# Two-layer decode attention on one core: PE's loop from step 1, the order of layouts and wo matmuls in step 31, and the type of the last transpose

## The chip, the core and the metric

The kernel runs on one core of a Trainium2 chip. The core has a matrix engine (TensorE, PE in the profile; its weight loads are the rows PEld), a vector engine (VectorE, DVE), a scalar engine (ScalarE, ACT), GpSimd (POOL) and a synchronisation engine (SyncE, SP) that here issues nearly all transfers. 16 DMA engines move data between memory (HBM) and the on-chip SBUF; each transfer is spread over all of them. PE writes its results to PSUM, from where DVE and ACT read them. The metric is device time of one execution in microseconds (us), given as a median of several runs; less is better.

## The reference

Two independent attention layers, A and B, each decode one token (one query row) against a cache of 8192 keys and values in 32 heads of 128. Their results are put side by side.

```python
D, H, Sk, Dh = 512, 32, 8192, 128          # for A and for B alike
q = (x @ wq).reshape(1, 1, H, Dh)           # x: 1 x 512, wq: 512 x 4096
scores = einsum("bhqd,bhkd->bhqk", q, k_cache) * Dh ** -0.5
p = softmax(scores, axis=-1)
o = einsum("bhqk,bhkd->bhqd", p, v_cache)
y = o.reshape(1, 1, H * Dh) @ wo            # wo: 4096 x 512
out = concatenate([y_A, y_B], axis=-1)      # 1 x 1024
```

All inputs and the output are bf16. The caches of both layers together are 268 MB, and the profile counts 285.21 MB read from HBM.

## The kernel before

A step `n` handles two heads of one layer: steps 0 to 15 are A's 32 heads, steps 16 to 31 are B's. The 128 partitions hold the two heads, 64 partitions each; a partition holds 128 keys of 128 elements. K and V of a step are one transfer of 4 MB each (`load_k`, `load_v`, issued on SP; V of step 31 in two halves), into two K buffers and two V buffers. K of step n+2 waits until PE has read K of step n (`red_done`), V of step n+2 until PE has used V of step n (`pv_done`).

One step goes through these operations, with the lines at which the profile shows them:

- `plan_mul` (L292, DVE): four multiplications of K, in place, by the query.
- `plan_red` (L301, PE): two groups of 16 matmuls with the identity, 512 columns each, which add up the products of a key into PSUM (`rps`); `plan_sr` (L310, DVE) finishes the sum to one score per key.
- `plan_max`, `plan_gmax` (L316, L322, L325): the maximum per head; `plan_exp` (L335 on PE, L339 and L346 on ACT) spreads it over the partitions and takes the exponentials.
- in the following step: `plan_sum` (L351, PE; L354, DVE) adds up the exponentials of the step before and takes the reciprocal; `plan_pv` (L367, PE) multiplies them with V in 128 matmuls of two columns; `plan_o` (L377, DVE) scales the result into `oD`.

So PE's order in step n is: sum of step n-1, reduction of step n, first half of the product with V of step n-1, maximum of step n, second half of that product, spread of step n. A last pass, step 32, has only the sum and the product of step 31.

The projection with wq (`plan_q`, L274 on PE, L282 on ACT) stands at the beginning for A and at the beginning of step 1 for B.

The projection with wo needs the result in another arrangement. `plan_relayout(a, g)` makes it for a group of heads: DVE writes a masked copy `zb` (L402), one PE matmul with a selection matrix turns it into `misc` (L406), DVE copies that to `o2` (L408). `plan_wo(a, g)` (L419, PE) then multiplies with the group's part of wo, four matmuls of one column per head, all 32 heads adding into `qyp`. A's 32 heads are one group; B's are groups of 16, 8, 4, 2 and 2 heads. A's layout and wo matmuls and the first three layouts of B stand at the head of step 31; B's last two layouts follow `plan_o` of steps 30 and 31, B's wo matmuls come at the very end. A's wo lies in the buffer `wbuf` from step 12 on. B's wo is loaded into the same buffer in five transfers (`load_wo`), which SP issues once A's wo matmuls are done (`wo_done[0]`). `plan_y` (L426, DVE) copies a layer's result to `yT`, for A behind the second multiplication of step 31. `plan_out` turns both with one PE matmul against the identity (L430), DVE copies the result (L433) and SP stores it.

The order on each engine is the order in which the plan's functions are called. `_Plan.op` appends an instruction to an engine's list, `_Plan.wait` a wait for a semaphore's count, left out when the engine has already waited for that count or a higher one. Four engines get their lists written out. PE's list is cut at `marks`: steps below `L0` are written out, steps `L0` to `L1 - 1` become a loop with two steps per round (`_emit_loop`), and the rest is written out again. In the loop a wait whose count grows from round to round is made against a register that is raised each round. With `L0 = 3` and `L1 = 31` these are 14 rounds, and every round must have the same instructions and waits.

Of the kernel before, what the change touches and what calls it, by code (L numbers as in the profile page):

```python
# [8 lines left out]
BF16 = mybir.dt.bfloat16  # L9
F32 = mybir.dt.float32  # L10

P = 128
# [11 lines left out]
class _Plan:  # L24
# [6 lines left out]
    def wait(self, eng, mark):  # L31
        if mark is None:
            return
        ctr, val = mark
        if val <= 0 or self.waited.get((eng, ctr.name), 0) >= val:
            return
        self.waited[(eng, ctr.name)] = val
        self.prog[eng].append((None, ctr, val))

    def op(self, eng, fn, ctr=None, needs=(), inc=1):  # L40

        for m in needs:
            self.wait(eng, m)
        self.prog[eng].append((fn, ctr, inc))
        if ctr is None:
            return None
        ctr.n += inc
        return ctr, ctr.n


def _emit(e, items):
    for fn, ctr, k in items:
        if fn is None:
            e.wait_ge(ctr.sem, k)
        elif ctr is None:
            fn(e)
        else:
            fn(e).then_inc(ctr.sem, k)


def _emit_loop(e, rounds):


    body = rounds[0]
    for r in rounds[1:]:
        assert len(r) == len(body)
        for (f0, c0, k0), (f1, c1, k1) in zip(body, r):
            assert (f0 is None) == (f1 is None) and c0 is c1
            assert f0 is None or k0 == k1
    grow = [rounds[1][i][2] - it[2] if it[0] is None else 0 for i, it in enumerate(body)]  # L70
    for n, r in enumerate(rounds):
        for it, d, base in zip(r, grow, body):
            assert it[0] is not None or it[2] == base[2] + n * d
    regs = {}
    for i, d in enumerate(grow):
        if d:
            regs[i] = e.alloc_register("w%d" % i)
            e.reg_mov(regs[i], body[i][2])
    with e.Fori(0, len(rounds)):
        due = []  # L80
        for i, it in enumerate(body):
            if i in regs:
                e.wait_ge(it[1].sem, regs[i])
                due.append(i)
                continue
            _emit(e, [it])
            if it[0] is not None:
                for j in due:
                    e.reg_add(regs[j], regs[j], grow[j])
                due = []  # L90
        for j in due:
            e.reg_add(regs[j], regs[j], grow[j])


def bass_concat_heads__mha_block_cached__gqa_block_cached__decode_kernel(
# [18 lines left out]
    NA = 2  # L114
# [22 lines left out]
    with ExitStack() as st:  # L137
# [3 lines left out]
        def sb(name, shape, dt):  # L141
            return ec(nc.sbuf_tensor(name, shape, dt))
# [14 lines left out]
        ident = sb("ident", [P, P], BF16)  # L157
        ident_f = sb("ident_f", [P, P], F32)
# [9 lines left out]
        mask = {g: sb("mask%d" % g, [P, P // g], BF16) for g in RG}  # L168
        jsel = {g: sb("jsel%d" % g, [P, g], BF16) for g in RG}
        NQ = NOUT // P  # L170
        yT = sb("yT", [P, NA, NQ], F32)
        out_q = sb("out_q", [NA * NQ, P], BF16)

        def ps(name, shape):
# [9 lines left out]
        pl = _Plan()  # L184
# [15 lines left out]
        def dma(eng, dst, src, c, needs=()):  # L200
            return op(eng, lambda e: e.dma_start(dst, src), c, needs, inc=16)  # L201


        def const(fn, needs=()):
# [5 lines left out]
            out=ident[:], in_=ones_bf[:], pattern=[[1, P]], compare_op=ALU.is_equal,  # L210
            fill=0.0, base=0, channel_multiplier=-1), [i_onesb])
        i_identf = const(lambda e: e.affine_select(
            out=ident_f[:], in_=ones_f[:], pattern=[[1, P]], compare_op=ALU.is_equal,
# [52 lines left out]
        def plan_q(a, j):  # L266

            def mm(e):
                r = None
                for hh in range(2):  # L270
                    for c in range(C):
                        w = wq_sb[a][:, c, 8 * j * Dh:8 * (j + 1) * Dh].rearrange(
                            "p (i h d) -> p i h d", h=2, d=Dh)[:, :, hh, :]
                        r = e.matmul(  # L274
                            qyp[hh * HP:(hh + 1) * HP, :].rearrange("p (i d) -> p i d", d=Dh),
                            xb[:, a, c, hh * HP:(hh + 1) * HP], w,
                            start=(c == 0), stop=(c == C - 1))
                return r
            m = op("PE", mm, c_pe, [x_ready, wq_in[a], qy_free[0]])
            q_done[a] = m  # L280
            n0 = a * PA + 4 * j
            qy_free[0] = op("ACT", lambda e: e.copy(  # L282
                qbc[:, n0:n0 + 4, :].rearrange("p i d -> p (i d)"), qyp[:]), c_act, [m])
            for n in range(n0, n0 + 4):
                qbc_ready[n] = qy_free[0]
# [110 lines left out]
        def plan_relayout(a, g):  # L396
            h0, n = WOG[a][g]
            z = z_n[0] % 2
            z_n[0] += 1
            s = P // n  # L400
            zv = zb[:, z, :].rearrange("p (h s) -> p h s", s=s)
            m = op("DVE", lambda e: e.tensor_tensor(  # L402
                zv, oD[:, a, h0:h0 + n].unsqueeze(2).broadcast_to([P, n, s]),
                mask[n][:, None, :].broadcast_to([P, n, s]), ALU.mult),
                c_dve, [sel_ready[n], o_done[a * PA + (h0 + n) // 2 - 1], z_free.get(z)])
            z_free[z] = op("PE", lambda e: e.matmul(misc[:, 0:n], zb[:, z, :], jsel[n][:],  # L406
                                                    start=True, stop=True), c_pe, [m, misc_free[0]])
            o2_ready[a, g] = misc_free[0] = op("DVE", lambda e: e.tensor_copy(  # L408
                o2[:, a, h0:h0 + n], misc[:, 0:n]), c_dve, [z_free[z]])

        def plan_wo(a, g):

            h0, n = WOG[a][g]

            def mm(e):
                r = None
                for j in range(h0, h0 + n):
                    for i in range(NQ):
                        r = e.matmul(qyp[:, i:i + 1], wo_sb[:, j, i * P:(i + 1) * P],  # L419
                                     o2[:, a, j:j + 1], start=(j == 0 and i == 0),  # L420
                                     stop=(j == H - 1 and i == NQ - 1), skip_group_check=True)
                return r
            wo_done[a] = op("PE", mm, c_pe, [o2_ready[a, g], wo_in[a, g], qy_free[0]])

        def plan_y(a):
            qy_free[0] = op("DVE", lambda e: e.tensor_copy(yT[:, a, :], qyp[:, 0:NQ]), c_dve,  # L426
                            [wo_done[a]])

        def plan_out():
            m = op("PE", lambda e: e.matmul(bmp[0:NA * NQ, 0:P], yT[:].rearrange("p a q -> p (a q)"),  # L430
                                            ident_f[:], start=True, stop=True),
                   c_pe, [qy_free[0], nb_done[NP - 1]])
            m = op("DVE", lambda e: e.tensor_copy(out_q[:], bmp[0:NA * NQ, 0:P]), c_dve, [m])  # L433
            done = dma("SP", out[0].rearrange("o (q n) -> (o q) n", q=NA * NQ), out_q[:], s_out, [m])
            wait("SP", done)


        L0, L1 = 3, 31
        marks = {}

        load_wq(0)
# [5 lines left out]
        for n in range(NP + 1):  # L447
            marks[n] = len(pl.prog["PE"])
            last = n == NP
            if n == L1:  # L450
                plan_relayout(0, 0)
                plan_wo(0, 0)
                for g in range(3):
                    plan_relayout(1, g)
            if n + 1 < NP:
                load_k(n + 1)
            if n == 1:
                for j in range(4):
                    plan_q(1, j)
            if not last:  # L460
                load_v(n, 2 if n == NP - 1 else 1)
            if n == 12:
                load_wo(0, 0)
            if n == NP - 1:
                for g in range(len(WOG[1])):
                    load_wo(1, g)
            if not last:
                plan_mul(n, 0)
                plan_mul(n, 1)
            if n == L1:  # L470
                plan_y(0)
            if n > 0:
                plan_sum(n - 1)
            if not last:
                plan_red(n, 0)
                plan_mul(n, 2)
                plan_mul(n, 3)
                plan_sr(n, 0)
                plan_red(n, 1)
            if n > 0:  # L480
                plan_pv(n - 1, 0, HT)
            if not last:
                plan_sr(n, 1)
                plan_max(n)
                plan_gmax(n)
            if n > 0:
                plan_pv(n - 1, HT, T)
            if not last:
                plan_exp(n)
            if n > 0:  # L490
                plan_o(n - 1)
            if n >= L1:
                plan_relayout(1, n - L1 + 3)
# [44 lines left out]
```

## Time and profile before

| | |
|---|---|
| median of three runs | 675.33 us (673.68, 675.33, 675.58) |
| the profiled execution's own time | 675.39 us |
| its span, first to last instruction | 673.7 us |
| HBM read | 285.21 MB, 423 GB/s over the span |
| busy: PE matmuls, PE weight loads | 469.2 us (70%), 275.7 us (41%) |
| busy: DVE, ACT, POOL | 359.5 us (53%), 43.9 us (7%), 2.1 us |
| mean granted clock of PE | 0.744 of full speed |
| chain that ended last | DMA 61%, PE 26%, DVE 8%, issue 4% |

How to read it: the span is what the profiler saw between the first and the last instruction; the time adds 1.7 us around it. A share of busy time is a mean over the whole span. The chain that ended last is followed back from the last instruction, at each step to what released it; its shares say where the time of that one chain lay. "issue" in it is time in which an engine waited for nothing that the profile shows. In timeline rows the brackets tell how long an engine had been idle before an instruction, and whose end released it. A transfer's time to landing counts from its issue on SP, so it includes the time behind other transfers.

### The profile page before, as it was taken

The numbers are of one execution on the slowest core, as the hardware profiler recorded it, in microseconds if no ns is written. First come the engines' busy times: TensorE is split into PE (matmuls) and PEld (weight loads), VectorE is DVE, ScalarE is ACT, GpSimd is POOL, SyncE is SP. The second block draws the span as 40 slices with busy tenths as digits, with TensorE's granted clock in tenths as the row PEclk, the third lists the DMA queues.
The fourth block names the chain that finished last, engine by engine and source line by source line (L and its number), as shares of the span: only waits on it lengthen the run. The fifth ranks groups of instructions, "written<-read, shape, count | busy, mean of one in ns | idle before, by whom it ended". The sixth has DMA issues, their size and how long they took to land.

```text
span 673.7 us, 12421 instructions
## 1 busy us (share of the span) xinstructions
PE 469.2 (70%) x5712; PEld 275.7 (41%) x5712; DVE 359.5 (53%) x345; ACT 43.9 (7%) x171; POOL 2.1 (0%) x13
## 2 busy tenths in 40 slices
PE   2665887667678766665677787766768875666977
PEld 1223444344444433442344444434444442344637
DVE  1553556566555665615655555656555565655361
ACT  1120000000000000000000000000000000000000
POOL 1000000000000000000000000000000000000000
PEclk9997877666787766776667887766788776678765
DMA  9999999999999999999999999999999999999994
GB/s 374 436 435 431 435 427 426 427 432 436 432 432 434 428 434 426 434 434 434 430 430 432 430 430 434 434 434 432 426 436 428 432 434 432 430 434 427 432 423 182
DMA packets 10547, 285.43 MB, mean 424 GB/s; under 512 B 1186, under 2 KB 1188, under 8 KB 1572
## 3 DMA queue, kind: packets, MB, share of 16 engines
q1 hardware_dynamic: 10528, 285.22, 98.6%
q8 instruction: 10, 0.16, 0.1%
q14 instruction: 5, 0.04, 0.0%
q10 hardware_dynamic: 4, 0.00, 0.0%
HBM read 285.21 MB, written 0.00 MB: 423 GB/s over the span
## 4 chain that ended last, share of the span: by engine, by line
DMA 61%; PE 26%; DVE 8%; issue 4%; ACT 0%; SPq 0%; ACTq 0%
DMA kn<-in_A_k_cache_dram 31%; DMA kn<-in_B_k_cache_dram 30%; PE rps L301 23%; DVE kn L292 7%; PE acc L367 1%; PE qyp L419 1%; PE bmp L335 0%; ACT pt L346 0%; PE misc L406 0%; DVE zb L402 0%; DVE o L408 0%; PE mtp L322 0%; PE bmp L430 0%; PE misc L351 0%; SPq L201 0%
## 5 line engine op out<-in xcount | busy, mean ns | idle before, releaser
L301 PE MATMUL rps<-kn,ident 128*128 128x512 bf16 x1024 | 292.3, 456 | 143.3 <-DVE kn L292 143.3
L292 DVE TENSOR_TENSOR kn<-kn,qbc 128x4096 bf16<-128x4096 bf16 x128 | 286.8, 2284 | 92.1 <-DMA kn<-in_A_k_cache_dram 62.1
L301 PEld LDWEIGHTS rps<-kn,ident 128*128 128x128 bf16 x1024 | 113.6, 114 | 309.7 <-DVE kn L292 141.9
L367 PEld LDWEIGHTS acc<-pt,vn 128*128 128x128 bf16 x4096 | 110.6, 97 | 14.3 <-issue 6.9
L310 DVE TENSOR_REDUCE s_sb<-rps 128x64 f32<-128x512 f32 x64 | 44.3, 692 | 131.2 <-PE rps L301 131.2
L367 PE MATMUL acc<-pt,vn 128*128 128x2 bf16 x4096 | 112.9, 164 | 0.0
L351 PE MATMUL misc<-rsum,ones_f 128*128 128x2 f32 x64 | 18.2, 354 | 39.2 <-ACT pt L346 38.8
L339 ACT ACTIVATE negb<-bmp 128x1 f32<-128x1 f32 x32 | 5.5, 171 | 594.5 <-PE bmp L335 594.5
L351 PEld LDWEIGHTS misc<-rsum,ones_f 128*128 128x128 f32 x64 | 15.5, 300 | 42.2 <-ACT pt L346 41.4
L377 DVE TENSOR_TENSOR oD<-acc,rinv 128x2 bf16<-128x2 f32 x32 | 5.1, 160 | 47.7 <-PE acc L367 47.7
L346 ACT ACTIVATE pt<-s_sb,negb 64x128 bf16<-64x128 f32 x64 | 27.9, 435 | 1.8
L335 PE MATMUL bmp<-gm,hrow 1*128 1x1 f32 x128 | 23.9, 287 | 0.5 <-DVE gm L325 0.5
L325 DVE TENSOR_REDUCE gm<-mtp 1x2 f32<-1x128 f32 x32 | 8.9, 279 | 27.8 <-PE mtp L322 27.8
L335 PEld LDWEIGHTS bmp<-gm,hrow 1*128 1x128 f32 x128 | 21.2, 233 | 1.3 <-issue 0.7
L322 PE MATMUL mtp<-ident_f,m 128*1 128x128 f32 x64 | 12.1, 271 | 1.1 <-DVE m L316 1.1
L274 PE MATMUL qyp<-wbuf,xb 128*64 128x512 bf16 x32 | 7.7, 633 | 6.3 <-DMA wbuf<-in_A_wq_dram 4.3
L346 ACT ACTIVATION_READ_ACCUMULATOR pt<-s_sb,negb 64x1 f32 x64 | 11.7, 182 | 0.0
L316 DVE TENSOR_REDUCE m<-s_sb 128x1 f32<-128x128 f32 x32 | 9.2, 287 | 1.1
L419 PE MATMUL qyp<-o,wbuf 128*128 128x1 bf16 x256 | 7.1, 165 | 0.3 <-DVE o L408 0.3
L419 PEld LDWEIGHTS qyp<-o,wbuf 128*128 128x128 bf16 x256 | 7.0, 104 | 0.4 <-DVE o L408 0.4
L274 PEld LDWEIGHTS qyp<-wbuf,xb 128*64 128x64 bf16 x32 | 2.4, 158 | 11.0 <-issue 6.3
L354 DVE RECIPROCAL rinv<-misc 128x2 f32<-128x2 f32 x32 | 5.3, 165 | 1.6 <-PE misc L351 1.6
(34 smaller groups left out, 29.1 us busy)
## 6 DMA issues: line engine op xcount, KB each, us to landing
kn<-in_A_k_cache_dram SPq DMA_DIRECT2D x16, 4096.0 KB, 25.5
vn<-in_A_v_cache_dram SPq DMA_DIRECT2D x16, 4096.0 KB, 31.5
kn<-in_B_k_cache_dram SPq DMA_DIRECT2D x16, 4096.0 KB, 25.2
vn<-in_B_v_cache_dram SPq DMA_DIRECT2D x15, 4096.0 KB, 31.4
wbuf<-in_A_wq_dram SPq DMA_DIRECT2D x1, 4096.0 KB, 12.2
vn<-in_B_wq_dram SPq DMA_DIRECT2D x1, 4096.0 KB, 30.7
wbuf<-in_A_wo_dram SPq DMA_DIRECT2D x1, 4096.0 KB, 40.8
vn<-in_B_v_cache_dram SPq DMA_DIRECT2D x2, 2048.0 KB, 18.1
```

The lines of the kernel that those rows point to most:

```text
L274: r = e.matmul(qyp[hh * HP:(hh + 1) * HP, :].rearrange("p (i d) -> p i d", d=Dh), xb[:, a, c, hh * HP:(hh + 1) * HP], w, start=(c == 0), s ...
L292: mul_done[n, c] = op("DVE", lambda e: e.tensor_tensor(k, k, qbc[:, n:n + 1, :].broadcast_to([P, CT, Dh]), ALU.mult), c_mul, [k_in[n], qbc ...
L301: r = e.matmul(rps[:, h, :].rearrange("p (t d) -> p t d", d=DW), ident[:], kn[:, n % NK, h * HT:(h + 1) * HT, i * DW:(i + 1) * DW], start= ...
L310: sr_done[n, h] = op("DVE", lambda e: e.tensor_reduce(s_sb[:, n % 2, h * HT:(h + 1) * HT], rps[:, h, :].rearrange("p (t d) -> p t d", d=DW ...
L316: m_done[n] = op("DVE", lambda e: e.tensor_reduce(m1[:, n % 2:n % 2 + 1], s_sb[:, n % 2, :], AX.X, ALU.max), c_dve, [sr_done[n, 1]])
L322: m = op("PE", lambda e: e.matmul(mtp[0:1, 0:P], m1[:, n % 2:n % 2 + 1], ident_f[:], start=True, stop=True), c_pe, [m_done[n], i_identf, g ...
L325: gm_done[n] = op("DVE", lambda e: e.tensor_reduce(gm[:, n % 2, :], mtp[0:1, 0:P].rearrange("o (h p) -> o h p", h=2), AX.X, ALU.max), c_dv ...
L335: r = e.matmul(bmp[:, 0:1], hrow[0:1, h, :], gm[0:1, n % 2, h:h + 1], start=(h == 0), stop=(h == 1))
L346: p_done[n] = op("ACT", lambda e, h=h, q=q: e.activation(pt[q, n % 2, :, h], s_sb[q, n % 2, :], AF.Exp, bias=negb[q, n:n + 1], scale=scale ...
L351: m = op("PE", lambda e: e.matmul(misc[:, 0:2], ones_f[:], rsum[:, n % 2, :], start=True, stop=True), c_pe, [p_done[n], misc_free[0]])
L367: r = e.matmul(acc[:, n % 2, 0:2], vn[:, n % NV, t, :], pt[:, n % 2, t, :], start=(t == 0), stop=(t == T - 1))
L419: r = e.matmul(qyp[:, i:i + 1], wo_sb[:, j, i * P:(i + 1) * P], o2[:, a, j:j + 1], start=(j == 0 and i == 0), stop=(j == H - 1 and i == NQ ...
```

## The change

Three edits are made together.

1. `L0` becomes 1: PE's loop covers steps 1 to 30, in 15 rounds, and steps 1 and 2 are no longer written out. `marks[1]` is set again behind B's `plan_q`, so that those matmuls stay in front of the loop. Since the first of these rounds does not have the same waits as the later ones, `_emit_loop` now groups the waits with the instruction that follows them (`_steps`), takes the waits of the later rounds, and carries their counts back to the first round; a wait that only the first round has is put in front of the loop.
2. At the head of step 31, `plan_wo(0, 0)` moves behind the three layouts of B.
3. `yT` becomes bf16, and the last transpose uses the bf16 identity in place of the f32 one.

```diff
+def _steps(items):
+    out, waits = [], []
+    for it in items:
+        if it[0] is None:
+            waits.append(it[1:])
+        else:
+            out.append((waits, it))
+            waits = []
+    assert not waits
+    return out
+
 def _emit_loop(e, rounds):
-    body = rounds[0]
...
+    rounds = [_steps(r) for r in rounds]
+    assert len({len(r) for r in rounds}) == 1
+    early, body = [], []
+    for k in range(len(rounds[0])):
+        at = [r[k] for r in rounds]
+        assert all(it[1:] == at[0][1][1:] for _, it in at)
+        first, second, third = at[0][0], at[1][0], at[2][0]
+        waits = []
+        for (ctr, v), (_, w) in zip(second, third):
+            d = w - v
+            assert v - d >= 1
+            waits.append((ctr, v - d, d))
+        for n, (ws, _) in enumerate(at[1:], 1):
+            assert [(c, v) for c, v in ws] == [(c, v + n * d) for c, v, d in waits]
+        for ctr, v in first:
+            same = [x for c, x, _ in waits if c is ctr]
+            if not same:
+                early.append((None, ctr, v))
+            else:
+                assert v <= same[0]
+        body.append((waits, at[0][1]))
+    _emit(e, early)
...
     with e.Fori(0, len(rounds)):
-        due = []
-        for i, it in enumerate(body):
...
+        for k, (waits, it) in enumerate(body):
+            for i, (ctr, v, d) in enumerate(waits):
+                e.wait_ge(ctr.sem, regs.get((k, i), v))
             _emit(e, [it])
+            for i, (ctr, v, d) in enumerate(waits):
+                if d:
+                    e.reg_add(regs[k, i], regs[k, i], d)
...
-        yT = sb("yT", [P, NA, NQ], F32)
+        yT = sb("yT", [P, NA, NQ], BF16)
...
             m = op("PE", lambda e: e.matmul(bmp[0:NA * NQ, 0:P], yT[:].rearrange("p a q -> p (a q)"),
-                                            ident_f[:], start=True, stop=True),
+                                            ident[:], start=True, stop=True),
                    c_pe, [qy_free[0], nb_done[NP - 1]])
...
-        L0, L1 = 3, 31
+        L0, L1 = 1, 31
...
             if n == L1:
                 plan_relayout(0, 0)
-                plan_wo(0, 0)
                 for g in range(3):
                     plan_relayout(1, g)
+                plan_wo(0, 0)
             if n + 1 < NP:
                 load_k(n + 1)
             if n == 1:
                 for j in range(4):
                     plan_q(1, j)
+                marks[n] = len(pl.prog["PE"])
```

## The prediction

> **What bounds the kernel now.** First the page's slices of the span: the DMA engines carry 426 to 436 GB/s in nearly every slice, and fall off only in the last.
>
> ```profile
> GB/s 374 436 435 431 435 427 426 427 432 436 432 432 434 428 434 426 434 434 434 430 430 432 430 430 434 434 434 432 426 436 428 432 434 432 430 434 427 432 423 182
> ```
>
> So up to about 662 us the stream of K and V sets the pace: a step takes 19.4 us, and VectorE (DVE) waits for each K tile. What can be won without moving fewer bytes lies behind the last K. So I read next the chain of work that ended last, in order of time, from the start of step 31 to the end (columns: start, length, engine with tile and line):
>
> ```profile
> 637.33 0.20 DVE o L408
> 637.53 0.05 issue
> 637.58 3.57 PE qyp L419 x128
> 641.15 0.05 PE misc L406
> 641.20 0.02 issue
> 641.23 0.17 DVE o L408
> ...
> 642.53 0.16 DVE o L408
> 642.69 0.78 DVE kn L292
> ...
> 647.15 9.66 PE rps L301 x32
> ...
> 663.28 3.43 PE acc L367 x128
> ...
> 667.47 3.43 PE qyp L419 x128
> ...
> 671.13 0.61 PE bmp L430 x2
> ```
>
> The reader is to see that the 128 matmuls with wo of A (L419, 3.57 us) stand in this chain ahead of step 31's multiplies (L292), although neither reads what the other writes. They are coupled by queue order: DVE's copy at 641.23 waits for the layout matmul L406, and that stands on TensorE (PE) behind L419. The same stretch in the timeline, then the issue of K of step 31 and, from the DMA view, how long it took to land, and the last piece of wo of B:
>
> ```profile
> 641.23 0.17 DVE L408 CAST o<-misc 128x16 bf16<-128x16 f32 x1 [3.50 <-PE misc L406]
> 642.61 4.48 DVE L292 TENSOR_TENSOR kn<-kn,qbc 128x4096 bf16<-128x4096 bf16 x2
> 647.15 9.66 PE L301 MATMUL rps<-kn,ident 128*128 128x512 bf16 x32 [3.75 <-DVE kn L292]
> ```
> ```profile
> 612.66 0.33 SPq L201 DMA_DIRECT2D kn<-in_B_k_cache_dram  x1
> ```
> ```profile
> kn<-in_B_k_cache_dram SPq DMA_DIRECT2D x1, 4096.0 KB, 24.8
> ```
> ```profile
> wbuf<-in_B_wo_dram SPq DMA_DIRECT2D x1, 256.0 KB, 23.0
> ```
>
> K of step 31 was there at 612.66 + 24.8 = 637.46, yet its first multiply began at 642.61: 5.15 us in which no DMA was waited for. The last wo piece was issued at 643.8 and landed at 666.8, so the stream ends 6.9 us ahead of the span.
>
> **The change, part by part.**
>
> *The layouts ahead of the matmuls with wo of A.* DVE's order of instructions stays as it is; only PE's order changes. DVE writes zb of B's group 0 at 637.44 already. From zb's start to its matmul the trace has 0.33 us (641.32 to 641.65), from there to the copy 0.22 (641.66 to 641.88). With L419 out of the way the matmul runs at 637.77 and the copy at 638.00 instead of 641.23: 3.23 us earlier. The next two groups keep their spacing of 0.65 us, so the first multiply begins at 639.38, still 1.92 us behind K's landing. Two multiplies of 4.48 together put the start of step 31's 32 reduction matmuls (L301) at 643.92 instead of 647.15.
>
> What the 3.57 us of L419 now stand beside: they start behind the last layout matmul (about 639.25) and end at 642.8. The sum of exponents (L351, 0.56) is queued behind them on PE and ends at 643.4, 0.5 us ahead of the reduction. That margin is the cover; whatever L419 runs late beyond it is paid one for one. On DVE the copy of A's result (L426) falls at 643.8 and waits for L419's end at 642.8; the reciprocal behind it waits for L351, at 643.4. Both are met. On SP the five loads of wo of B wait for L419: they go out from about 642.8 instead of 641.18. Nothing stands behind them on SP but the output. The engines are still on V of step 31 then, whose second half, issued at 636.6 and 20.4 us on its way, lands at 657.0; so a start 1.6 us later is hidden by 14 us of backlog, and I leave wo's landings where they were.
>
> The reduction's 9.66 us depend on the clock. PE's granted clock in four half-microseconds of this tail (columns: stretch, length, PE busy with its instructions, clock, DMA share, GB/s):
>
> ```profile
> 640.00:640.50 0.50, 0.50 (x25) 0.50 1.06 459
> 649.00:649.50 0.50, 0.50 (x3) 0.50 1.15 492
> 652.50:653.00 0.50, 0.50 (x4) 1.00 0.77 328
> 665.50:666.00 0.50, 0.50 (x24) 0.50 0.06 25
> ```
>
> Matmuls of one or two columns leave the clock at 0.50 though PE is busy throughout (0.50 of 0.50 us, at 640 and 665.5); the 512-column ones brought it up 5.3 us after their start. With L419 now directly ahead of the reduction I therefore expect the same cold start, and 9.66 again. The reductions of all steps from 2 on lie between 8.38 and 9.99 by the phase of the switching: -1.3 to +0.3 for the range.
> The Trainium skill, in "TensorE: Matmul & The Clock Gate", section "Part 1: The HAM clock gate (the "warmup" mystery)", says that some 3.4 us of sustained PE activity lift the clock; by that, 3.57 us of L419 right ahead would make the reduction start fast, and 32 matmuls at the 0.227 us that the trace shows for one at full clock in step 1 would take 7.3 us, some 2.4 less, of which the landing of wo would leave 0.6. The row at 665.5, inside a long busy stretch at 0.50, decides against it here.
>
> Behind the reduction the chain keeps its order. The product with V of step 31 (L367) moves from 663.28 to 660.05; V's halves land at 652.1 and 657.0. The matmuls with wo of B move from 667.47 to 664.24. The pieces land from 661.9 (641.18 + 20.7) to 666.8; the last eight matmuls are reached at 664.24 + 120 x 0.0268 = 667.45, 0.6 us behind the landing. So the full 3.23 arrives at the end; gains above some 3.85 us here would meet that landing.
>
> *The result turned in bf16.* L430 takes two passes in f32; from its start to the next operation are 0.63 us. The nearest rows are the bf16 layout matmuls L406: 0.24 for 32 columns, 0.22 to 0.23 for 4 and 8, so 0.32 at 128 by that slope. That gains 0.31, on the chain. Ends: 0.2 if columns cost twice the slope, 0.4 if they cost nothing. The copy into yT (0.16) matches a copy to bf16 (0.16): nothing.
>
> *PE's loop from step 1.* Steps 1 and 2 become the 15th round; no matmul is added. Waits of the first round are carried back from the later ones: the sum L351 of step 1 now waits until ScalarE's four copies of plan_q are done, which is 45.37 + 0.58 = 45.95, against a start of 45.25. DVE's reciprocal took it at 46.56, so 46.4 at its end is soon enough. Behind that PE has the reduction, on which the K load of step 3 waits (SP, 54.83); V of step 1, issued at 45.37, is then in front of it for another 18 us. What a jump into the loop and back costs is seen where the loop is now, at L351 in step 2 (straight), 3 (entry) and 5 (after a jump back):
>
> ```profile
> 60.49 0.59 PE L351 MATMUL misc<-rsum,ones_f 128*128 128x2 f32 x2 [1.30 <-ACT pt L346]
> 82.44 0.59 PE L351 MATMUL misc<-rsum,ones_f 128*128 128x2 f32 x2 [1.30 <-ACT pt L346]
> 120.57 0.59 PE L351 MATMUL misc<-rsum,ones_f 128*128 128x2 f32 x2 [1.30 <-ACT pt L346]
> ```
>
> All three are equal: nothing, and DVE's 4.69 us of idle before K of step 2 (63.28) cover an entry that does cost. Fewer instructions to fetch: page part 3 has 10 packets, 0.16 MB, in q8. By the records of the 16 part-landings a packet holds back the one engine that carries it by 1.2 to 1.5 us, and a transfer counts when its last part lands. The engine that was last at the end (3.2 us behind the first) was made so by q14's packets, not by these, so fewer of them move nothing. Bounds: -1.2 (the last engine loses a packet) to +1.2 (it gets one); I take 0.
> The Trainium skill, in "Runtime: NRT & Kernel Launch", section "Instruction fetch mechanics", warns that a taken branch out of the fetched window stalls for a fetch. It prices nothing; the equal 1.30 us say that here it is hidden.
>
> **Sum.** 3.23 + 0.31 = 3.54. The profiled execution took 675.39 us, its span 673.7, and 1.7 lies around it; it is 0.06 above the median of 675.33. So the span becomes 670.2 and the median 671.8.
>
> **Rivals.**
> 1. *The gain is cut.* The wo pieces land as late as they are issued (+1.6), or L419 holds up the reduction. The last matmuls would be met at 668.4 instead of 667.45: 1.0 lost, 672.8; with both about 674. For it: margins of only 0.5 and 0.6 us. Against: the backlog to 657.
> 2. *No change, about 675.3.* The multiplies wait for K after all, or the stream's end decides. It needs K to land 5.1 us later against the step before, where the last three K tiles landed 19.43 and 19.44 us apart. It would also be so if the order on PE made no difference, which the wait of 3.50 speaks against.
> 3. *Slower: fetching.* If PE has to fetch the loop body anew in its rounds from its new place, each of the 15 brings packets. Each costs 1.2 us if it falls on the engine that is last. Three such packets eat the 3.54; from five on (6.0 against 3.54 + 2.0) the kernel is slower; six give 679. Against: 14 rounds now show only 10 packets in all, and the body is the same two steps.
>
> **How the numbers follow.** Forecast 0.73, rival 1 0.12, rival 2 0.07, rival 3 0.08. A change under 0.3% (2.0 us) can't be told from none. The forecast ends below 673.3 nearly always; rival 1 does so in half of its cases: faster 0.77. Same takes the other half and rival 2: 0.14. Slower 0.09. The forecast's low end is the clock's gain up to wo's landing (0.6) and a lost packet (1.2): 670.0. Upward, clock (+0.3), packet (+1.2) and 0.1 of L430 give 673.4; rival 1 takes it to 674.0. Range 670.0 to 674.0.
>
> **What would show it.** Right: L408 of B's group 0 ends no idle of 3.5 us; L419 stands between L406 x4 and L351; the first multiply of step 31 begins 1.9 us behind K's landing; L301 follows with PE idle near 0.5 us and takes 8.4 to 10 us; the last L419 begins without waiting for DMA; one L430. Wrong: a DMA as releaser of those multiplies or of L419, L351 of steps 1 to 3 with more than 1.30 us behind ScalarE, or q8 with far more than 10 packets.

## The result and the profile after

The changed kernel takes 671.67 us (median of four runs, 671.43 to 672.0) against 675.46 us (673.68 to 675.77) for the kernel before: ratio 0.995, 95% interval 0.9932 to 0.9968, so 2.2 to 4.6 us less. The profiled execution took 671.82 us with a span of 670.0 us.

The page's rate of transfers by slice is what it was; the last slice, in which the stream has run out, is a fuller one:

```profile
GB/s 376 438 433 422 427 436 435 432 428 425 439 434 434 426 425 436 438 430 430 423 436 438 430 430 425 436 436 432 430 425 436 436 431 428 428 434 434 433 416 272
```

The chain that ended last, in order of time, from step 31 on. L427 is the layout matmul, L429 its copy, L440 the wo matmuls, L222 the issue of transfers, L447 the copy into `yT`, L451 the last transpose:

```profile
637.12 0.19 DVE o L429
...
637.56 0.21 PE misc L427
...
638.88 0.18 PE misc L427
639.06 3.43 PE qyp L440 x128
642.49 0.02 issue
642.51 0.33 SPq L222
...
645.18 21.87 DMA wbuf<-in_B_wo_dram
667.05 0.14 issue
667.19 0.37 PE qyp L440 x8
667.56 0.02 issue
667.58 0.17 DVE yT L447
667.75 0.04 issue
667.80 0.28 PE bmp L451
```

The multiplications, the reduction and the product with V of step 31 are no longer in it. It now runs through the load of B's wo: the last piece lands at 667.05, and the last eight of the 128 matmuls wait for it. The view puts that load behind A's wo matmuls and its issue on SP (L222), but a later issue does not make it land later: in `e7_after_double_wo_a` below the last piece was issued at 649.64 instead of 645.18 and landed at 666.89. So the landing goes with the stream ahead of it and not with the issue, as the prediction's backlog has it. The timeline of the same stretch:

```profile
638.92 3.55 PE L440 MATMUL qyp<-o,wbuf 128*128 128x1 bf16 x128
639.18 4.48 DVE L313 TENSOR_TENSOR kn<-kn,qbc 128x4096 bf16<-128x4096 bf16 x2
642.34 0.56 PE L372 MATMUL misc<-rsum,ones_f 128*128 128x2 f32 x2
643.72 9.34 PE L322 MATMUL rps<-kn,ident 128*128 128x512 bf16 x32 [0.82 <-DVE kn L313]
658.87 3.55 PE L388 MATMUL acc<-pt,vn 128*128 128x2 bf16 x128
663.05 3.79 PE L440 MATMUL qyp<-o,wbuf 128*128 128x1 bf16 x120
667.19 0.35 PE L440 MATMUL qyp<-o,wbuf 128*128 128x1 bf16 x8 [0.34 <-DMA wbuf<-in_B_wo_dram]
```

A's wo matmuls (638.92) now lie beside the multiplication (639.18) that they had held up, which begins 3.43 us earlier than in the kernel before. The product with V begins 4.28 us earlier (658.87 against 663.15), B's wo matmuls too (663.05 against 667.33). Yet those end only 3.33 us earlier, at 667.56 against 670.89: the other 0.95 us went into waiting for the load, some 0.5 at the last piece and 0.2 each at the two pieces before it, which stand inside the 3.79 us of the row with 120 matmuls. The rows of the kernel before that these are set against:

```profile
663.15 3.55 PE L367 MATMUL acc<-pt,vn 128*128 128x2 bf16 x128
667.33 3.55 PE L419 MATMUL qyp<-o,wbuf 128*128 128x1 bf16 x128
```

Of the instruction packets there are 8 in PE's queue instead of 10:

```profile
q8 instruction: 8, 0.13, 0.1%
q14 instruction: 5, 0.04, 0.0%
```

### The profile page after: what moved, and what is told of

The parts are those of the page before. It is cut to its first block, busy times and chain, and to the rows that moved or that the text cites. A ratio compares the mean times of both kernels' runs of the same rounds, so it can differ in the third digit from the quotient of the medians.

```text
span 670.0 us, 12431 instructions
## 1 busy us (share of the span) xinstructions
PE 473.1 (71%) x5711; PEld 276.2 (41%) x5711; DVE 359.6 (54%) x345; ACT 43.9 (7%) x171; POOL 2.1 (0%) x13
## 4 chain that ended last, share of the span: by engine, by line
DMA 65%; PE 23%; DVE 7%; issue 4%; SPq 0%
DMA kn<-in_A_k_cache_dram 31%; DMA kn<-in_B_k_cache_dram 30%; PE rps L322 22%; DVE kn L313 7%; DMA wbuf<-in_B_wo_dram 3%; PE qyp L440 1%; PE acc L388 0%; SPq L222 0%; PE bmp L356 0%; PE misc L427 0%; DVE zb L423 0%; DVE o L429 0%; PE mtp L343 0%; PE bmp L451 0%; DVE out_q L454 0%
## 5 line engine op out<-in xcount | busy, mean ns | idle before, releaser
L372 PE MATMUL misc<-rsum,ones_f 128*128 128x2 f32 x64 | 18.2, 355 | 39.5 <-ACT pt L367 38.8
L372 PEld LDWEIGHTS misc<-rsum,ones_f 128*128 128x128 f32 x64 | 15.5, 301 | 42.9 <-ACT pt L367 41.3
L356 PE MATMUL bmp<-gm,hrow 1*128 1x1 f32 x128 | 23.2, 282 | 0.5 <-DVE gm L346 0.5
L356 PEld LDWEIGHTS bmp<-gm,hrow 1*128 1x128 f32 x128 | 20.6, 226 | 1.3 <-issue 0.7
L295 PE MATMUL qyp<-vn,xb 128*64 128x512 bf16 x32 | 6.6, 554 | 2.3 <-ACT qbc L303 2.3
L440 PE MATMUL qyp<-o,wbuf 128*128 128x1 bf16 x256 | 7.6, 165 | 0.5 <-DMA wbuf<-in_B_wo_dram 0.3
L440 PEld LDWEIGHTS qyp<-o,wbuf 128*128 128x128 bf16 x256 | 7.2, 104 | 0.7 <-issue 0.4
```

What stands on the lines that cost most here:

```text
L295: r = e.matmul(qyp[hh * HP:(hh + 1) * HP, :].rearrange("p (i d) -> p i d", d=Dh), xb[:, a, c, hh * HP:(hh + 1) * HP], w, start=(c == 0), s ...
L356: r = e.matmul(bmp[:, 0:1], hrow[0:1, h, :], gm[0:1, n % 2, h:h + 1], start=(h == 0), stop=(h == 1))
L372: m = op("PE", lambda e: e.matmul(misc[:, 0:2], ones_f[:], rsum[:, n % 2, :], start=True, stop=True), c_pe, [p_done[n], misc_free[0]])
```

## Experiments

Theory at the outset: the order of PE in step 31 carries nearly all of the gain, the landing of B's wo cuts it, the bf16 transpose adds 0.3 us, the loop nothing. Rivals: the loop carries it by fewer packets; the landing is no bound. In the course a further theory was needed for the loop (theory F below). Each kernel stands beside executions of the kernel before on the same chip. The ratio compares the means of all executions; differences of medians come out up to 0.7 us away from it.

### Each edit alone

The order alone (`e1_order_only`):

```diff
                 plan_relayout(0, 0)
-                plan_wo(0, 0)
                 for g in range(3):
                     plan_relayout(1, g)
+                plan_wo(0, 0)
```

> The kernel before with edit 2 alone: A's wo matmuls behind the three layouts of B. Theory (the order carries nearly all of the gain, and the landing of B's last wo piece cuts it): the first multiplication of step 31 begins 3.2 us earlier than before, the last wo matmuls meet the landing, and the end misses only the 0.3 us of the bf16 turn: 672.0 us (671.5 to 672.5). Rival (the loop from step 1 carries it, by fewer instruction fetches and so an earlier stream): no more than 0.5 us faster than before, 675 us.

Measured: 672.59 us (671.96 to 673.25), ratio 0.9965 (0.995 to 0.9979): 2.4 us less than before (1.4 to 3.4). The theory's place is met: the chain ends with the landing of wo, at 667.41 here, and the f32 transpose behind it. The timeline shows one thing more:

```profile
662.60 0.38 PE L419 MATMUL qyp<-o,wbuf 128*128 128x1 bf16 x9
663.94 3.26 PE L419 MATMUL qyp<-o,wbuf 128*128 128x1 bf16 x111 [0.96 <-issue]
667.54 0.35 PE L419 MATMUL qyp<-o,wbuf 128*128 128x1 bf16 x8 [0.35 <-DMA wbuf<-in_B_wo_dram]
```

Behind the ninth of B's wo matmuls PE stands still for 0.96 us, with nothing in the profile that it waits for. Here it costs little, since the landing ends last anyway.

The transpose in bf16 alone (`e2_bf16_only`): `yT` in bf16, `ident` for `ident_f`.

> The kernel before with edit 3 alone. Theory: the last transpose takes one pass, from its start to the next operation 0.31 us instead of 0.63, and the time falls by 0.3 us, to 675.1, which cannot be told from no change by the time, but can in the trace. Rival (the f32 transpose is cheaper than it looks since its second pass lies beside something): 0.63 stays, 675.4 us.

Measured: 674.97 us (673.6 to 675.52), ratio 0.9996 (0.9986 to 1.0006), not told from no change by the time. In the trace the transpose starts at 671.31 and its copy at 671.62: 0.31 us, as expected. The gap is there again, and here nothing covers it:

```profile
666.43 0.38 PE L419 MATMUL qyp<-o,wbuf 128*128 128x1 bf16 x9
667.73 3.33 PE L419 MATMUL qyp<-o,wbuf 128*128 128x1 bf16 x119 [0.92 <-issue]
```

The loop from step 1 alone (`e3_loop_only`): `L0 = 1` with the new `_emit_loop`, everything else as before.

> The kernel before with edit 1 alone: the loop from step 1. Theory: no change in the time (675.4, within 0.7 us); 8 instruction packets in q8 instead of 10; the sum of exponentials in step 1 waits for ScalarE's copies of the query, and DVE still has idle time before K of step 2. Rival A (fewer packets bring the K tiles earlier): 674.2 us or less, K of step 31 landing 1.2 us earlier. Rival B (the carried-back wait in step 1 costs): 676 us or more, with K of step 3 issued late and no DVE idle time before it.

Measured: 673.37 us (672.25 to 675.5), ratio 0.9981 (0.9969 to 0.9993): 1.3 us less (0.5 to 2.1). The theory missed. Rival A is not the cause: K of step 31 landed at 637.37, against 637.46 before. Rival B is not either; the wait of the sum in step 1 for ScalarE is there, but is short:

```profile
46.09 0.38 PE L372 MATMUL misc<-rsum,ones_f 128*128 128x2 f32 x2 [0.70 <-ACT qbc L303]
63.02 4.49 DVE L313 TENSOR_TENSOR kn<-kn,qbc 128x4096 bf16<-128x4096 bf16 x2 [4.45 <-DMA kn<-in_A_k_cache_dram]
```

DVE still idles 4.45 us before K of step 2. What differs is the tail. In this profiled execution the two last reductions were quick (8.41 and 9.10 us against 9.99 and 9.66 before), which is the clock's phase; but B's wo matmuls ran in one piece, which in `e2_bf16_only` they did not:

```profile
664.17 3.55 PE L440 MATMUL qyp<-o,wbuf 128*128 128x1 bf16 x128
```

In the profiled execution of the kernel before they ran in one piece too (the row at 667.33 above): its reductions were slow, and PE came to these matmuls 0.9 us later than in `e2_bf16_only` (666.43). So the gap is not there in every execution, and whether it is what the loop gained has to be tested.

### Where PE's instruction packets end

Theory F: the gap is PE waiting for its next packet of instructions (8 packets are 0.13 MB, so 16 KB each); where a packet ends in the tail depends on the length of the program ahead of it, and the loop moved it to a harmless place. The Trainium skill, "Runtime: NRT & Kernel Launch", section "Instruction fetch mechanics", counts 256 instructions to a block of 16 KiB; in this case `e7_after_double_wo_a`, with 256 instructions more than the changed kernel, has 9 packets instead of 8. By the trace's records of packets, a packet of PE's queue ends 1.2 to 1.6 us ahead of the end of each such gap. Two kernels shift the packets by more matmuls at 8 us, ahead of the projection with wq: the kernel before with 46 (`e5_before_pad46`), and the loop alone with 82 in the same place (`e6_loop_pad82`). They push that projection back, from 13.15 us to 14.87 and 18.44, but not the stream: K of step 31 landed at 637.52 and 637.73.

```diff
-                for c in range(C):
+                for c in [0] * (46 if a == 0 else 0) + list(range(C)):
```

> The kernel before with 46 more matmuls (92 PE instructions with their weight loads) ahead of the two that spread x, at 8 us, where PE waits for wq anyhow; they write what is written again at once. This shifts the 256-instruction packets of PE's program to where they fall, in the tail, in the kernel with the loop from step 1. Theory F (what the loop alone gained, 673.37 against 675.35, comes from where a packet boundary falls in the tail: with the long program PE ran out at the ninth matmul of the last wo group sequence, a gap of 0.92 and 0.96 us called issue in the runs of the turn alone and of the order alone): no such gap, and 673.4 us (672.6 to 674.2). Rival L (the shorter program or the fewer packets gained it): 675.3 us as before. Rival P (the loop alone was only lucky in the phase of the clock): 675.3 us too.

> The loop from step 1 alone, with 82 more matmuls (164 PE instructions) in the same place, which puts the packet boundary back to the ninth matmul of the last wo matmuls. Theory F: 675.0 to 675.4 us, the gain of the loop is gone, and a gap called issue of up to 0.95 us near that matmul where the reductions were quick. Rival L: 673.4 us as without the matmuls. Rival P: anything between 673.4 and 675.4, with no such gap.

Measured: with 46, 673.32 us (672.89 to 675.29), ratio 0.9986 (0.9976 to 0.9996), 0.9 us less and within the interval of the loop's gain, without the loop, and B's wo matmuls in one piece of 3.55 us. With 82, 674.13 us (673.47 to 675.3), ratio 0.9994 (0.9985 to 1.0003): no gain clear of noise over the kernel before beside it (674.61), and the gap behind the ninth matmul, at the very matmul where it was expected:

```profile
664.91 0.38 PE L440 MATMUL qyp<-o,wbuf 128*128 128x1 bf16 x9
665.60 3.34 PE L440 MATMUL qyp<-o,wbuf 128*128 128x1 bf16 x119 [0.32 <-issue]
```

So the place of the gap goes with the place of the packet's end. The loop is not needed for a gain of this size, nor is a shorter program (the first of the two is longer than the kernel before). That the loop's own gain is all of this kind is likely but not shown: the intervals with 46 and with 82 matmuls overlap, the gap was 0.32 us and not 0.9, and the time 674.13 and not 675. The size of the gap varies with when the packet comes, which these runs do not settle.

### Does the landing of B's wo end last?

The changed kernel without the loads of B's wo (`e4_after_no_wo_b`):

```diff
                 for g in range(len(WOG[1])):
-                    load_wo(1, g)
+                    wo_in[1, g] = wo_in[0, 0]
```

> The changed kernel without the five loads of wo of B (4 MB); the matmuls stay and read A's wo instead, so B's half of the output is another. Theory (in the changed kernel the landing of B's wo sets the end): the last wo matmuls start without a wait and end 3.45 us after the first, about 1.0 us earlier against the chain than in the changed kernel: 670.6 us (670.2 to 671.1), give or take the clock's phase in the last reduction. Rival (the chain of compute sets the end and the landing only happens to fall there): 671.6 us as with the loads.

Measured: 670.62 us (669.43 to 672.22), ratio 0.9926 (0.9909 to 0.9942): 1.05 us under the changed kernel by the medians, as the theory has it; but with four executions each the two intervals against the kernel before overlap, so the time alone does not show it. The traces do: the last eight matmuls wait for the last piece in the changed kernel (0.34 us), in `e1_order_only` (0.35) and in the second profile of the changed kernel (`e9_after_again`, 0.35). The spread fits: 2.8 us here, 0.6 us with the loads (1.9 in the later set). Without the landing at the end, a quick or slow reduction would show in the time; with it, the landing cuts off what a quick reduction gains. The profiled execution was the slowest of the four (reductions of 9.93 and 9.54 us); its B matmuls began at 664.12 and ran in one piece.

### How much cover A's wo matmuls have

Each of them issued twice, in the changed kernel (`e7_after_double_wo_a`):

```diff
-                for j in range(h0, h0 + n):
+                for j in [j for j in range(h0, h0 + n) for _ in range(2 - a)]:
```

> The changed kernel with each of A's wo matmuls issued twice, so that A's half of the output comes out about double. Theory (A's wo matmuls are covered by the two multiplications with 0.8 us to spare, and beyond that are paid for until the landing of B's wo is no longer what ends last): 3.43 us more on PE delay the last reduction by 2.6, of which some 1.0 goes into the time that PE now waits for the landing: 673.2 us (672.4 to 674.0). Rival (these matmuls lie beside other work altogether): 671.7 us.

Measured: 674.56 us (673.67 to 676.44), ratio 0.9998 (0.9988 to 1.0009). That is 1.4 us more than the theory had, and the timeline tells why:

```profile
637.68 3.79 PE L440 MATMUL qyp<-o,wbuf 128*128 128x1 bf16 x137
643.72 3.31 PE L440 MATMUL qyp<-o,wbuf 128*128 128x1 bf16 x119 [2.25 <-issue]
646.89 0.56 PE L372 MATMUL misc<-rsum,ones_f 128*128 128x2 f32 x2
647.32 3.15 PE L322 MATMUL rps<-kn,ident 128*128 128x512 bf16 x7
```

The 256 instructions more brought a packet's end into this stretch, and PE stood for 2.25 us. From the start of A's wo matmuls to the sum L372 are now 9.21 us instead of 3.42, so 5.79 more. The reduction would have begun at 637.93 + 4.54 = 642.47 (start of the multiplications, and their distance to the reduction in the changed kernel) and began at 647.32, 4.85 late. The cover is the difference, 0.9 us. The theory's mechanism holds, with its margin of 0.8; its sum lacked the gap. How large the gap was in the other executions is not known.

### A kernel with fewer DVE instructions

By the trace's records of the 16 part-landings of a transfer, the last part comes 3.3 to 3.5 us behind the first at the last wo piece of the changed kernel's two profiles, and 1.2 to 1.5 us behind the next to last. The distance from first to last part grew from 2.4 to 3.4 us at a packet of 8 KB in queue q14 at 540 us; further such packets ran at 107, 184, 326 and 620 us. `e8_lean_dve` has 287 DVE instructions in its trace instead of 412:

```diff
-    CT = 32
+    CT = 64
...
-                plan_mul(n, 0)
-                plan_mul(n, 1)
+                plan_mul(n, 0)
...
-                plan_mul(n, 2)
-                plan_mul(n, 3)
-                plan_sr(n, 0)
+                plan_mul(n, 1)
+                if n >= NP - 2:
+                    plan_sr(n, 0)
...
-                plan_sr(n, 1)
+                if n >= NP - 2:
+                    plan_sr(n, 1)
+                else:
+                    plan_sr2(n)        # one tensor_reduce over both banks
...
                 rinv[:, n, :], misc[:, 0:2]), c_dve, [m])
+            wait("DVE", r_done[n])
```

> The changed kernel with fewer DVE instructions, 286 instead of 412 by the trace's count: two multiplications of 8192 columns per step instead of four of 4096, one sum over both banks of the reduction instead of two in steps 0 to 29, and the wait for the reciprocal put ahead of the second multiplication. Theory (the last wo piece lands late because one DMA engine carries DVE's instruction packets, at 105, 324 and 538 us, some 1.2 us each): two such packets instead of three, the last of the 16 part-landings 2.3 us behind the first instead of 3.5, the last wo piece at 665.9 instead of 667.05, and 670.6 us (670.2 to 671.1). Rival (the late engine is late for another reason): landing at 667.0, 671.7 us.

Measured: 670.83 us (670.49 to 670.93), ratio 0.9939 (0.9926 to 0.9952). The last wo piece landed at 666.06 instead of 667.05, its last part 2.4 us behind the first. The end of a packet of PE's queue is now in B's wo matmuls again, and in this profile it is what ends last, not the landing:

```profile
663.62 0.93 PE L446 MATMUL qyp<-o,wbuf 128*128 128x1 bf16 x29 [0.65 <-DMA wbuf<-in_B_wo_dram]
665.54 1.07 PE L446 MATMUL qyp<-o,wbuf 128*128 128x1 bf16 x35 [0.99 <-issue]
```

To rule out the chip, this kernel and the changed one were run side by side.

> The changed kernel itself, beside the leaner one on the same chip. Every theory: 671.7 us (671.3 to 672.2), with a small spread, since the landing of B's wo ends last.

> The leaner kernel again, with two packets of DVE's instructions instead of three. Theory (the late DMA engine carries them): 670.8 us (670.3 to 671.2), 0.8 to 0.9 us below the changed kernel beside it, and the last wo piece about 1.0 us earlier. Rival (the difference between the first two measurements was one of the chip): no difference within 0.3 us.

Measured: 671.87 us (671.39 to 673.27; ratio 0.9958, 0.9945 to 0.9972) for the changed kernel, 670.92 us (670.72 to 671.66; ratio 0.9943, 0.9929 to 0.9957) for the lean one. The last wo piece landed at 667.19 and 665.97; the last part was 3.5 and 2.4 us behind the first. By medians the lean kernel is 0.95 us faster than the changed one; the two intervals against the kernel before overlap, and the landing times carry the reading better than the medians do. The next to last part landed at 665.80 and 665.66 in the first pair, at 665.72 and 665.69 in the second: it is the latest part that moved. The packets of q14 moved too, from 107, 326 and 540 us to 150 and 470, while those near 183 and 621 stayed, so those three go with DVE's program. That the pieces were issued 1.1 to 2.0 us earlier in the lean kernel is no rival: in `e7_after_double_wo_a` an issue 4.5 us later left the landing where it was. That DVE's packets make the engine late is borne out by the landing moving as forecast; which engine carries them is not in the profile, and the lean kernel's other merges could have helped to bring the end forward.

## Why the prediction was right, and where it was not

The forecast was 671.8 us, a gain of 3.54 by the profiled execution; measured were 671.67 and, between the two profiled spans, 3.7.

- **The order.** The layout of B's group 0 was forecast to run at 637.77 and the first multiplication at 639.38; they ran at 637.56 and 639.18, both 0.2 earlier since step 31 itself began 0.21 earlier (copy of A's layout at 637.12 instead of 637.33). K of step 31 landed at 637.64, so the multiplication waited for no DMA. Shown, here and in `e1_order_only`.
- **The cover of A's wo matmuls.** Forecast: they end at 642.8 and the reduction follows with 0.5 us to spare. Measured: the sum behind them ends at 642.90, the reduction begins at 643.72 with PE 0.82 us idle, and the doubled matmuls give a cover of 0.9.
- **The clock.** Forecast: the reduction starts slow although A's wo matmuls stand right ahead, and takes 9.66 us again. It took 9.34. The windows of PE's clock (stretch, length, PE busy, clock, DMA share, GB/s) show the slow start, full clock 4.6 us later, and the product with V:

```profile
642.00:642.50 0.50, 0.50 (x19) 0.50 1.07 459
644.00:644.50 0.50, 0.50 (x2) 0.50 1.37 590
648.50:649.00 0.50, 0.50 (x4) 1.00 1.01 426
659.00:659.50 0.50, 0.50 (x25) 0.50 0.93 393
661.50:662.00 0.50, 0.50 (x25) 0.50 1.10 446
```

The rule of the Trainium skill, "TensorE: Matmul & The Clock Gate", section "Part 1: The HAM clock gate (the "warmup" mystery)", that some 3.4 us of sustained PE activity lift the clock, fails here for matmuls of one and two columns. A's wo matmuls in the changed kernel cannot show it: by the trace's records the clock changed only on a grid of 3.41 us, with steps at 638.10 and 641.51, and their 3.55 us from 638.92 on filled no interval of it. But the product with V filled the one from 658.58 to 661.99 (PE busy 3.41 of 3.41 us, the last two rows above), and the clock stayed at 0.50 to the end. In `e3_loop_only` A's wo matmuls filled the one from 635.50 to 638.91, and the clock stayed at 0.50 until 649.16, in the reduction. So the forecast's choice was right; its row at 665.5 was also inside an interval that PE filled but for 0.04 us (662.66 to 666.07).
- **The landing of B's wo.** Forecast: the last matmuls reach their piece 0.6 us behind its landing, and gains above 3.85 us would meet it. By the clock's phase the chain came 4.28 us earlier instead of 3.23 (0.2 from the earlier start of step 31, 0.3 in its reduction, 0.5 in the steps behind it, where L356 took 0.60 us and L335 before 1.00), and the landing, 0.2 later than in the kernel before, took 0.95 of it back: L440's last eight matmuls did wait for DMA, against the forecast's list of signs. The landing ends last in both profiled executions of the changed kernel. That it does so in most others is the likely reason why the median met the forecast so closely, and is not shown: the landing lay between 666.8 and 667.4 us in the nine profiles with these loads and the old DVE program, while B's wo matmuls began between 664.17 and 667.33 in the five of them with the old order. So the forecast's 3.23 was right at its place, and at the end right within 0.1 only by luck: two things of about 1 us, a quicker clock and the wait for the landing, nearly cancelled.
- **The transpose.** Forecast 0.32 us from its start to the next operation; measured 0.31 (667.80 to 668.11).
- **The loop.** "I take 0" was wrong for the loop by itself: alone it gained 1.3 us (0.5 to 2.1 by the interval). The step that failed is the one that weighed fewer packets only by what they do to the data stream. It overlooked that PE can run out of instructions in the tail, behind the ninth of B's wo matmuls, and that two steps less of written-out program move that point; `e5_before_pad46` gains 0.9 us by moving it without the loop, and `e6_loop_pad82` brings the gap back. That this is all of the 1.3 is not shown. What the loop adds in the changed kernel cannot be told: the edits alone give 2.4 + 0.3 + 1.3 = 4.0 us and all three together 3.4, by the same ratios, a difference well inside the intervals. Nothing was lost at the loop's jump back, where L372 starts 1.30 us behind ScalarE as before (81.96), nor at its entry, which is now step 1: 0.69 us behind ScalarE, as in the straight matmuls of plan_q just ahead of it.
- **The carried-back wait in step 1** was forecast to be met in time. In `e3_loop_only` it was (DVE's reciprocal at 46.55). In the changed kernel's profiled execution PE was at half clock from 40.8 us on, in the middle of plan_q (in `e3_loop_only` at full clock), and DVE waited 1.93 us there and had only 0.66 us left before K of step 2:

```profile
48.72 0.17 DVE L375 RECIPROCAL rinv<-misc 128x2 f32<-128x2 f32 x1 [1.93 <-PE misc L372]
62.98 4.49 DVE L313 TENSOR_TENSOR kn<-kn,qbc 128x4096 bf16<-128x4096 bf16 x2 [0.66 <-DMA kn<-in_A_k_cache_dram]
```

Nothing was lost, K still ended last, but of the slack of 4.69 us that the prediction named 4.45 were there in `e3_loop_only` and only 0.66 in this execution.

## What to carry to other kernels

Where a stream of transfers sets the pace, look for the gain in the chain behind the last input, and there for work that stands in a queue ahead of something that does not need it; then find what lands last, since that cuts the gain. Work out each edit against that floor and not by adding up the edits: here the chain came 4.28 us earlier at the last matmuls and 3.33 of them were left at their end. When a queue's instruction count changes, even far ahead, look in the tail for gaps with no releaser at multiples of the packet size.

## What the runs showed of the hardware that was not expected

- PE can run out of instructions. With nothing that it waits for in the profile it stood 0.96, 0.92, 0.32 and 0.99 us in B's wo matmuls (order alone, transpose alone, padded loop, lean kernel), 0.37 and 0.66 in the second profiles of the changed and the lean kernel, and 2.25 us in the doubled ones of A; shifting the program by 92 or 164 instructions removed the gap or brought it back to the same matmul. Packets of 16 KB took 0.9 to 1.2 us each. The Trainium skill, "Runtime: NRT & Kernel Launch", section "Instruction fetch mechanics", calls the cost of crossing a boundary of 16 KiB "mostly hidden"; in this tail of narrow matmuls at 27 ns, where 256 instructions last 3.5 us, it was not.
- Instruction packets also cost the data stream: a transfer's 16 parts landed within 0.8 us of each other at the start and 3.0 to 3.8 us apart at the end (2.4 in the lean kernel), the largest steps, of 1.0 to 1.5 us, at the times of packets. With one DVE packet less the last landing came 1.0 and 1.2 us earlier.
- Within one execution PE's granted clock changed only on a grid of 3.41 us, and the grid's phase differed from execution to execution; the last two reductions lay between 8.4 and 10.0 us, which goes with the phase. Kernels without a landing at the end spread over 1.5 to 3.3 us (four sets of the kernel before, loop alone, no wo of B); the changed and the lean kernel, which in three of their four profiles end with a landing, stayed within 0.4 to 0.9 in three of their four sets of runs and 1.9 in the fourth. How much of the spread is the phase alone is not shown.
